# The tail of a decode kernel: down weights in longer runs, and the last 64 rows spread over other transfer engines

## The chip, the cores and the metric

One core of one Trainium2 chip runs the kernel. The metric is device time in microseconds (us) of one execution, median of several. Each timed execution also has a span, from the first to the last instruction that the profile records; the time is 1.7 us or more longer than the span.

The time before was 684.42 us (three runs, 684.41 to 684.58).

## The reference, cut to what matters

One decode step, one token, width 640: adaptive layer norm, attention over a cache of 16,384 positions in 32 heads of 128, then a second layer norm and a gated feed-forward part of width 1,728.

```python
g = silu(h @ w_gate)          # (640) @ (640, 1728)
u = h @ w_up
x = x + gb * ((g * u) @ w_down)   # (1728) @ (1728, 640)
```

The caches are 2 x 32 x 16,384 x 128 bf16, 268 MB of the 290 MB that the kernel reads. Everything else is small, but the feed-forward weights come last, and the output can't be stored until the last row of `w_down` is in and multiplied.

## The kernel before

1,728 = 13 x 128 + 64. The product with `w_down` takes 13 blocks of 128 rows and a rest of 64. Row blocks are loaded in pairs: partition p gets two neighbouring rows of 640 bf16, one run of 2,560 bytes. The columns of gate and up must then be taken in the same order, every second one, so that block j of `gu` meets block j of `w_down`.

```python
NPR = FJ // 2                                    # FJ = 13, FR = 64
wd_cut = [(0, 3), (3, 5), None, (5, NPR), NPR]   # blocks 0-5, 6-9, rest, 10-11, 12
for n, c in enumerate(wd_cut):
    if c is None:
        dst, src = wdr_v[0:FR], B_wd[128 * FJ:F, :]          # 64 rows on partitions 0 to 63
    elif c == NPR:
        dst, src = wd_v[:, 2 * NPR, :], B_wd[256 * NPR:128 * FJ, :]
    else:
        dst = wd_v[:, 2 * c[0]:2 * c[1], :].rearrange("p (q i) n -> p q (i n)", i=2)
        src = B_wd[256 * c[0]:256 * c[1], :].rearrange("(q p i) n -> p q (i n)", p=128, i=2)
    d_wd.append(plan.dma(...))                   # all on the sync queue, after w_gate and w_up
# ... cut: attention output, layer norm, h2 ...
def f_gu(e, wv, ps_t):                           # gate (wv = w_gate), then up (wv = w_up)
    for j in range(FCH):
        for k in range(KC):                      # KC = 5
            if j < 2 * NPR:
                w = wv[:, k, 256 * (j // 2):256 * (j // 2 + 1)].rearrange("p (m i) -> p i m", i=2)[:, j % 2, :]
            else:
                w = wv[:, k, 128 * j:min(F, 128 * (j + 1))]
            r = e.matmul(ps_t[...], lhsT=w, rhs=h2_col[:, k:k + 1], ...)
# ... cut: silu, gu = silu(gate) * up ...
for n, c in enumerate(wd_cut):                   # one PE group for each load, in this order
    o_dn = op(PE, ..., lambda e: f_down(e, js, ...), deps=[o_gum, d_wd[n], o_zf, o_dn])
```

Of the kernel before, what the change touches and what calls it, by code (L numbers as in the profile page):

```python
# [36 lines left out]
class _Plan:  # L37
# [21 lines left out]
    def op(self, eng, pos, fn, deps=(), name=""):  # L59
        o = _Op(eng, pos, fn, list(deps), name, len(self.ops))  # L60
        self.ops.append(o)
        return o
# [89 lines left out]
def build(nc, A_x, A_k, A_v, A_wq, A_wo, B_wg, B_wu, B_wd, c_in, w_mod, out):  # L152
    H, S, Dh = A_k.shape[1], A_k.shape[2], A_k.shape[3]
    D = A_x.shape[2]
    F = B_wg.shape[1]
    KC = D // 128
    TT = S // 128
    FJ = F // 128
    FR = F - 128 * FJ
# [5 lines left out]
    NI = H // 2  # L165
# [14 lines left out]
    with es:  # L180
        block = es.enter_context(nc.Block())
        plan = _Plan(nc, es)
# [17 lines left out]
        wd_v = flat1[:, 2 * KC * F:2 * KC * F + FJ * D].rearrange("p (j n) -> p j n", j=FJ)  # L200
        wdr_v = flat1[:, 2 * KC * F + FJ * D:2 * KC * F + FCH * D]
# [88 lines left out]
        def f_cols(e, v):  # L290
            r = None
            row = cx_row[:, v, :].rearrange("o (m j) -> o j m", j=KC)
            for k in range(KC):
# [6 lines left out]
                  deps=[o_xcol], name="x_f32")  # L300
# [31 lines left out]
        def layernorm_ops(pos, src_f32, src_dep, c0, tag, xc_t):  # L332
# [22 lines left out]
            deps=[o_xc, o_rstd, o_onep], name="t1")  # L355
# [43 lines left out]
        o_fold = [[] for _ in range(NI)]  # L399
# [17 lines left out]
        for i in range(NI):  # L417
# [11 lines left out]
            if 2 * i % G == 0:  # L429
                d_wo[g] = plan.dma(qpos["wo", g], woring[:],  # L430
                                   A_wo[g * G * 128:(g + 1) * G * 128, :].rearrange("(g p) n -> p g n" if lastg else "(p g) n -> p g n", g=G), "wo",
                                   deps=[o_wo[G * g - 1]] if g >= 1 else [], name="dma_wo%d" % g)
            r0 = base - 12.0 if i > 0 else 2.5
            def f_qbc(e, s2=s2, heads=heads):
# [9 lines left out]
                deps=[o_qbcmm[i], o_mult[i - 2] if i >= 2 else None], name="qbc%d" % i)  # L444

            qb = qbc_sb[:, s2].unsqueeze(1).broadcast_to([128, TC, 128])
            for c in range(NC):
# [3 lines left out]
                               deps=[d_k[i], o_qbc[i], o_gm[i - 1] if i >= 1 else None], name="mult%d_%d" % (i, c))  # L451
# [3 lines left out]
                def f_fold(e, sh=sh, ks=ks):  # L455
# [9 lines left out]
                    deps=[o_fold[i][c], o_exp[i - 1] if i >= 1 else None], name="red%d_%d" % (i, c)))  # L465
# [9 lines left out]
            for b in range(2):  # L475
# [3 lines left out]
                    deps=[o_nb[i], o_zrs, o_pvlast[i - NP] if i >= NP else o_zp] + o_red[i], name="exp%d_%d" % (i, b))  # L479
            if last:  # L480
# [9 lines left out]
                               name="dma_v%d_%d" % (i, n)) for n, (a, b) in enumerate(vcut if last else [(0, TP)])]  # L490

            def f_pv(e, j0, j1, i=i, s2=s2, sp=sp, jl=(NG * 3 // 4 if last else NG)):
                r = None
                for j in range(j0, j1):
# [7 lines left out]
                       deps=[o_exp[i], d_v[i][0], o_acc[i - 2] if i >= 2 else (o_xf, o_modc)[i], o_cc], name="pva%d" % i)  # L502
# [3 lines left out]
                          deps=[o_pvb, o_diag[i - 1] if i >= 1 else None], name="acc%d" % i)  # L506

            if not last:

                def f_orow(e, s2=s2, hc=hc):  # L510
# [12 lines left out]
                    deps=[o_rl[i], o_tr[i - 2] if i >= 2 else None], name="O_row%d" % i)  # L523
# [15 lines left out]
                if lastg or heads[1] % G == G - 1:  # L539
                    oc = hc if lastg else slice(heads[1] + 1 - G, heads[1] + 1)  # L540
                    o_on[i] = op(ACT, vbase + 1.2, lambda e, oc=oc: e.activation(out=On[:, oc], in_=OT_ps[:, oc], func=ACTF.Copy),  # L541
                                 deps=[o_tr[i]], name="on%d" % i)
# [34 lines left out]
        QE = float(len(order)) + 1.0  # L577
# [1 line left out]
        d_wu = plan.dma(QE + 0.01, wu_v, B_wu.rearrange("(p k) n -> p k n", k=KC), "wu", deps=[o_fold[NI - 1][-1]], name="dma_wu")  # L579


        NPR = FJ // 2
        wd_cut = [(0, 3), (3, 5), None, (5, NPR), NPR]
        d_wd = []
        for n, c in enumerate(wd_cut):
            if c is None:
                dst, src = wdr_v[0:FR], B_wd[128 * FJ:F, :]
            elif c == NPR:
                dst, src = wd_v[:, 2 * NPR, :], B_wd[256 * NPR:128 * FJ, :]
            else:  # L590
                dst = wd_v[:, 2 * c[0]:2 * c[1], :].rearrange("p (q i) n -> p q (i n)", i=2)
                src = B_wd[256 * c[0]:256 * c[1], :].rearrange("(q p i) n -> p q (i n)", p=128, i=2)
            d_wd.append(plan.dma(QE + 0.02 + 0.01 * n, dst, src, ("wd", n), deps=[o_fold[NI - 1][-1]], name="dma_wd%d" % n))

        o_abf = op(ACT, TE, lambda e: e.activation(out=attn_bf[:], in_=attn_ps[:, 0:KC], func=ACTF.Copy), deps=[o_wo[H - 1]], name="attn_bf")  # L595
# [1 line left out]
                  deps=[o_abf, o_modc], name="ga_attn")  # L597
        o_x1 = op(DVE, TE + 0.2, lambda e: e.scalar_tensor_tensor(
            out=x1[:], in0=tt2[:], scalar=1.0, in1=x_f32[:], op0=ALU.mult, op1=ALU.add, accum_out=st[:, 8:9]),
            deps=[o_ga, o_xf], name="x1")  # L600
# [3 lines left out]
            deps=[o_xc1, o_rstd1, o_onep_b, o_h], name="t2")  # L604
        o_h2 = op(DVE, TE + 1.1, lambda e: e.tensor_tensor(out=h2_col[:], in0=tt1[:], in1=mod_col[:, 3 * KC:4 * KC], op=ALU.add),
                  deps=[o_t2], name="h2_col")
# [4 lines left out]
        def f_gu(e, wv, ps_t):  # L611
            r = None
            for j in range(FCH):
                for k in range(KC):
                    if j < 2 * NPR:
                        w = wv[:, k, 256 * (j // 2):256 * (j // 2 + 1)].rearrange("p (m i) -> p i m", i=2)[:, j % 2, :]
                    else:
                        w = wv[:, k, 128 * j:min(F, 128 * (j + 1))]
                    r = e.matmul(ps_t[0:(128 if j < FJ else FR), j:j + 1], lhsT=w, rhs=h2_col[:, k:k + 1],
                                 start=(k == 0), stop=(k == KC - 1))  # L620
            return r
        o_g = op(PE, TE + 1.2, lambda e: f_gu(e, wg_v, g_ps), deps=[o_h2, d_wg, o_zg], name="gate")
        o_u = op(PE, TE + 1.25, lambda e: f_gu(e, wu_v, u_ps), deps=[o_h2, d_wu, o_zu], name="up")
        o_eg = op(ACT, TE + 1.3, lambda e: e.activation(out=eg[:], in_=g_ps[:, 0:FCH], func=ACTF.Exp, scale=-1.0), deps=[o_g], name="eg")
        o_dg = op(DVE, TE + 1.4, lambda e: e.tensor_scalar_add(out=dg[:], in0=eg[:], scalar1=1.0), deps=[o_eg], name="dg")
# [20 lines left out]
        def f_down(e, js, first, fin):  # L646
            r = None
            for j in js:
                kw = 128 if j < FJ else FR
                wv = wd_v[:, j, :] if j < FJ else wdr_v[0:FR, :]  # L650
                for g in range(4):
                    r = e.matmul(f_ps[32 * g:32 * g + 1, 0:RW], lhsT=gu_col[0:kw, j:j + 1], rhs=wv[:, RW * g:RW * (g + 1)],  # L652
                                 start=(first and j == js[0]), stop=(fin and j == js[-1]), skip_group_check=True)
            return r
        o_dn = None
        for n, c in enumerate(wd_cut):
            js = [FJ] if c is None else ([2 * NPR] if c == NPR else list(range(2 * c[0], 2 * c[1])))
            o_dn = op(PE, TE + 1.8 + 0.01 * n, lambda e, n=n, js=js: f_down(e, js, n == 0, n == len(wd_cut) - 1),
                      deps=[o_gum, d_wd[n], o_zf, o_dn], name="down%d" % n)
        o_t3 = op(DVE, TE + 1.9, lambda e: e.tensor_tensor(out=t3_row[:], in0=f_ps[:, 0:RW], in1=gb_row[:], op=ALU.mult),  # L660
                  deps=[o_dn, o_gbr], name="gb_ffn")
# [8 lines left out]
def bass_adaLN_cond__gqa_block_cached__swiglu_ffn__decode_kernel(  # L670
    nc: bass.Bass,
    A_x: bass.AP,
    A_k_cache: bass.AP,
    A_v_cache: bass.AP,
    A_wq: bass.AP,
    A_wo: bass.AP,
    B_x: bass.AP,
    B_w_gate: bass.AP,
    B_w_up: bass.AP,
    B_w_down: bass.AP,  # L680
    c: bass.AP,
    w_mod: bass.AP,
    out: bass.AP,
):
    build(nc, A_x, A_k_cache, A_v_cache, A_wq, A_wo, B_w_gate, B_w_up, B_w_down, c, w_mod, out)
# [28 lines left out]
```

## Time and profile before

| what | before |
|---|---|
| time, median | 684.42 us |
| span of the profiled execution | 682.7 us |
| moved by the transfer engines | 290.81 MB, 426 GB/s |
| last w_up landing | 672.42 us |
| last w_down landing | 679.04 us |
| output store issued | 680.66 us |

Names in the lines below: PE is TensorE, the matrix engine, PEld its weight loads, DVE is VectorE, SPq the queue of SyncE that issues the loads; `kring` and `vbuf` are buffers that loads fill.

Two lines of the page of the kernel before: the busy share of the 16 transfer engines in 40 slices (9 is 90% or more), and the count of transfer packets by size.

```profile
DMA  9999999999999999999999999999999999999996
...
DMA packets 8082, 290.81 MB, mean 426 GB/s; under 512 B 826, under 2 KB 1532, under 8 KB 3196
```

The kernel is bound by its transfers up to the last slice. A change to the `w_down` loads can only gain in the last 14 us: their first packet starts at 668.46 us. The chain of waits that ended last, in the kernel before (start us, length us, what):

```profile
648.71 28.91 DMA kring<-in_B_w_down_dram
677.62 0.04 issue
677.67 0.73 PE psb L652 x15
678.40 0.14 issue
678.53 0.33 PE psb L652 x3
678.86 0.14 issue
679.00 0.47 PE psb L652 x8
679.46 0.14 issue
679.60 0.33 PE psb L652 x4
```

The chain waits for a `w_down` load that lands at 677.62, then runs four PE groups. The PE instructions of the tail in time order (start, length, line, operation, output and inputs, count, and in brackets the idle time before and what ended it); L619 is up, L652 the product with `w_down`:

```profile
672.47 2.25 PE L619 MATMUL psb<-h_col,kring 128*128 128x1 bf16 x70 [1.87 <-DMA kring<-in_B_w_up_dram]
675.99 0.97 PE L652 MATMUL psb<-kring,gu_col 128*1 128x160 bf16 x24 [1.27 <-DMA kring<-in_B_w_down_dram]
677.67 0.70 PE L652 MATMUL psb<-kring,gu_col 128*1 128x160 bf16 x16 [0.70 <-DMA kring<-in_B_w_down_dram]
678.53 0.30 PE L652 MATMUL psb<-kring,gu_col 64*1 64x160 bf16 x4 [0.16 <-PE psb L652]
679.00 0.43 PE L652 MATMUL psb<-kring,gu_col 128*1 128x160 bf16 x8 [0.16 <-PE psb L652]
679.60 0.30 PE L652 MATMUL psb<-kring,gu_col 128*1 128x160 bf16 x4 [0.17 <-PE psb L652]
```

The first two groups of `w_down` wait for transfers, the last three follow each other with gaps of 0.14 us. The trace also records when each of the 16 engines finished its share of each load. These are the last three of the sixteen (not a view of the page, but the landing records of the trace), and the instruction fetch in the same stretch with the first packets that follow it on its engine:

```
kernel before, landings in us, the three latest engines of 16
w_up               672.29  672.41  672.42
w_down blocks 0-5  674.82  674.83  675.86
blocks 6-9         676.55  676.64  677.62
rest of 64 rows    676.95  677.04  677.83
blocks 10-11       677.60  677.61  678.63
block 12           678.00  678.02  679.04

instruction fetch, 16,384 bytes   672.837 to 673.939
2,560-byte packet                 673.925 to 674.206
2,560-byte packet                 674.192 to 674.472
```

One engine is level with the others when up lands, and 1.03 us behind when the first `w_down` load lands. I call it the straggler. An instruction fetch took 1.10 us of one engine in this stretch, and the first two packets after it take 281 ns each in place of about 104. The trace does not number the engines; that the straggler is the engine of the fetch is tested below (more_130).

Last, three groups of PE matmuls of the kernel before, with one output column each (L555 has two), that differ in the step between the weight columns (busy us, then mean ns of one): L312 has a step of 5 elements, L619 of 2, L555 of 1.

```profile
L312 PE MATMUL psb<-silu_c,vbuf 128*128 128x1 bf16 x150 | 6.2, 178 | 7.1 <-DMA vbuf<-in_w_mod_dram 7.1
...
L619 PE MATMUL psb<-h_col,kring 128*128 128x1 bf16 x130 | 3.8, 165 | 3.7 <-DMA kring<-in_B_w_up_dram 1.9 <-DVE h_col L605 1.9
...
L555 PE MATMUL psb<-P_sb,vbuf 128*128 128x2 bf16 x64 | 1.8, 165 | 2.1 <-DMA vbuf<-in_A_v_cache_dram 2.1
```

The mean length includes the pipeline; the spacing of starts is 40 ns for L312 and 27 ns for the other two. L312 runs at the start of the kernel. L567, also with a step of 5, runs at 664.54 us, between L555 and L619, and has 40 ns too, so the place in the program is not what differs.

### The profile page before, as it was taken

How to read it: one execution, taken by the hardware profiler on the slowest of the kernel's cores; microseconds unless marked ns; L12 is line 12 of the kernel's file. 1: busy time of each engine (PE TensorE's matmuls, PEld its weight loads, DVE VectorE, ACT ScalarE, POOL GpSimd, SP SyncE). 2: the span in 40 equal slices, each digit the busy share in tenths (PEclk: the TensorE clock that was granted, in tenths of full speed). 3: DMA queues.
4: the chain of work that ended last, by engine and by line, in shares of the span. 5: the costliest groups of instructions: out<-in, count | busy, mean ns of one | idle time of the engine just before them, and what ended most of it. 6: DMA issues, size and time to landing. Idle time of an engine off the chain costs nothing.

```text
span 682.7 us, 5209 instructions
## 1 busy us (share of the span) xinstructions
PE 313.0 (46%) x2503; PEld 73.6 (11%) x2055; DVE 485.2 (71%) x254; ACT 55.5 (8%) x206; POOL 9.4 (1%) x30
## 2 busy tenths in 40 slices
PE   1504354554428270644527263462716345255744
PEld 1300010110102010010101001020100101001133
DVE  1029797979696894949589593968949495889901
ACT  1100101010100101010100101010010101001020
POOL 1000000000000000000000000000000000000000
PEclk9957676766858685675758557586755767568975
DMA  9999999999999999999999999999999999999996
GB/s 379 443 427 438 405 447 443 438 442 416 438 430 431 434 443 430 430 427 433 443 430 430 431 426 435 430 430 439 430 434 435 430 434 439 431 434 427 408 423 245
DMA packets 8082, 290.81 MB, mean 426 GB/s; under 512 B 826, under 2 KB 1532, under 8 KB 3196
## 3 DMA queue, kind: packets, MB, share of 16 engines
q1 hardware_dynamic: 8056, 290.48, 98.9%
q8 instruction: 18, 0.29, 0.2%
q14 instruction: 4, 0.03, 0.0%
q10 hardware_dynamic: 4, 0.00, 0.0%
HBM read 290.47 MB, written 0.00 MB: 425 GB/s over the span
## 4 chain that ended last, share of the span: by engine, by line
DMA 60%; DVE 27%; PE 8%; issue 2%; ACT 2%; SPq 1%; POOL 0%; DVEq 0%
DMA kring<-in_A_k_cache_dram 38%; DVE kring L450 17%; DMA vbuf<-in_A_v_cache_dram 14%; DVE kring L452 7%; DMA kring<-in_B_w_down_dram 4%; DMA kring<-in_A_v_cache_dram 4%; PE psb L377 3%; PE psb L496 3%; DVE S_sb L463 2%; PE psb L375 1%; ACT P_sb L476 1%; DVE pm L468 1%; PE psb L567 1%; SPq L71 1%; PE psb L652 0%
## 5 line engine op out<-in xcount | busy, mean ns | idle before, releaser
L450 DVE TENSOR_TENSOR kring<-kring,qbc_sb 128x8192 bf16<-128x8192 bf16 x64 | 282.7, 4418 | 105.6 <-DMA kring<-in_A_k_cache_dram 101.4
L377 PE MATMUL psb<-kring,ident 128*128 128x512 bf16 x448 | 162.7, 525 | 0.0
L452 DVE TENSOR_TENSOR kring<-kring 128x4096 bf16<-128x4096 bf16 x64 | 146.7, 2292 | 2.2
L375 PE MATMUL psb<-kring,ident 128*128 128x512 bf16 x64 | 33.0, 516 | 245.1 <-DVE kring L452 245.1
L496 PE MATMUL psb<-vbuf,P_sb 128*32 128x512 bf16 x944 | 75.0, 473 | 48.2 <-DMA vbuf<-in_A_v_cache_dram 48.1
L463 DVE TENSOR_REDUCE S_sb<-psb 128x64 f32<-128x512 f32 x64 | 43.8, 684 | 35.8 <-PE psb L377 35.8
L496 PEld LDWEIGHTS psb<-vbuf,P_sb 128*32 128x32 bf16 x944 | 26.9, 112 | 151.7 <-issue 84.8
L505 ACT ACTIVATE acc_sb<-psb 128x512 f32<-128x512 f32 x16 | 9.6, 597 | 395.2 <-PE psb L496 395.2
L375 PEld LDWEIGHTS psb<-kring,ident 128*128 128x128 bf16 x64 | 6.4, 101 | 316.7 <-DVE kring L452 306.0
L534 PE MATMUL psb<-ident,O_row 2*32 2x1 bf16 x112 | 4.2, 172 | 35.8 <-ACT O_row L521 35.8
L473 ACT ACTIVATE nb<-gm 64x1 f32<-64x1 f32 x32 | 6.4, 201 | 154.7 <-POOL gm L470 154.3
L476 ACT ACTIVATE P_sb<-S_sb,nb 64x256 bf16<-64x256 f32 x32 | 18.5, 578 | 0.8
L513 PE MATMUL psb<-acc_sb,sel 128*2 128x128 f32 x120 | 15.8, 276 | 0.0
L470 POOL PARTITION_ALL_REDUCE gm<-pm x16 | 5.7, 356 | 619.1 <-DVE pm L468 586.9
L468 DVE TENSOR_REDUCE pm<-S_sb 64x1 f32<-64x256 f32 x32 | 13.2, 414 | 0.8
L596 DVE TENSOR_TENSOR tt<-attn_bf,mod_col 128x5 f32<-128x5 bf16 x1 | 0.2, 165 | 14.2 <-ACT attn_bf L595 14.2
L513 PEld LDWEIGHTS psb<-acc_sb,sel 128*2 128x2 f32 x120 | 9.3, 85 | 2.4
L312 PE MATMUL psb<-silu_c,vbuf 128*128 128x1 bf16 x150 | 6.2, 178 | 7.1 <-DMA vbuf<-in_w_mod_dram 7.1
L567 PE MATMUL psb<-On,woring 128*128 128x1 bf16 x160 | 7.8, 179 | 3.0 <-ACT On L541 2.5
L567 PEld LDWEIGHTS psb<-On,woring 128*128 128x128 bf16 x160 | 7.1, 131 | 3.7 <-ACT On L541 3.2
L534 PEld LDWEIGHTS psb<-ident,O_row 2*32 2x32 bf16 x112 | 3.0, 111 | 38.5 <-ACT O_row L521 38.5
L336 DVE TENSOR_SCALAR xc<-x_f,st 128x5 f32<-128x5 f32 x1 | 0.2, 230 | 9.7 <-POOL st L333 9.7
(89 smaller groups left out, 87.7 us busy)
## 6 DMA issues: line engine op xcount, KB each, us to landing
kring<-in_A_wq_dram SPq DMA_DIRECT2D x1, 5120.0 KB, 26.6
woring<-in_A_wo_dram SPq DMA_DIRECT2D x8, 640.0 KB, 23.9
vbuf<-in_w_mod_dram SPq DMA_DIRECT2D x1, 4800.0 KB, 14.5
vbuf<-in_A_v_cache_dram SPq DMA_DIRECT2D x1, 4096.0 KB, 19.8
vbuf<-in_A_v_cache_dram SPq DMA_DIRECT2D x2, 2048.0 KB, 26.4
kring<-in_B_w_gate_dram SPq DMA_DIRECT2D x1, 2160.0 KB, 20.4
kring<-in_B_w_up_dram SPq DMA_DIRECT2D x1, 2160.0 KB, 25.2
kring<-in_B_w_down_dram SPq DMA_DIRECT2D x1, 960.0 KB, 28.2
```

What stands on the lines that cost most here:

```text
L375: return e.matmul(dst, lhsT=ident[:], rhs=rhs, start=True, stop=fin)
L377: return e.add_instruction(mybir.InstMatmult(name=nc.get_next_instruction_name(), engine=mybir.EngineType.PE, start_tensor_calc=False, sto ...
L450: o_mult[i] = op(DVE, base + 7.0 * c, lambda e, ks=ks, qb=qb: e.tensor_tensor(out=ks, in0=ks, in1=qb, op=ALU.mult), deps=[d_k[i], o_qbc[i] ...
L452: o_f1 = op(DVE, base + 7.0 * c + 4.4, lambda e, ks=ks: e.tensor_tensor(out=ks[:, :, 0:64], in0=ks[:, :, 0:64], in1=ks[:, :, 64:128], op=A ...
L463: o_red[i].append(op(DVE, base + 7.0 * c + 11.5 if c < NC - 2 else base + 7.0 * (NC - 1) + 4.5 + 0.1 * c, lambda e, sh=sh, c=c: e.tensor_r ...
L468: o_mx = op(DVE, eb + 0.1 * b, lambda e, i=i, b=b: e.tensor_reduce(out=pm[half[b], b:b + 1], in_=S_sb[half[b]], axis=AX.X, op=ALU.max), de ...
L476: o_exp[i] = op(ACT, eb + 0.6 + 0.1 * b, lambda e, i=i, b=b, sp=sp: e.activation(out=P_sb[half[b], sp, 0:2 * TP].rearrange("p (t b) -> p b ...
L496: r = e.matmul(acc_ps[s2][q4:q4 + 32, :], lhsT=P_sb[:, sp, 8 * j:8 * j + 32], rhs=vt[i][:, 4 * j:4 * j + 4, :].rearrange("p a d -> p (a d) ...
L505: o_acc[i] = op(ACT, pvb + 0.5, lambda e, s2=s2: e.activation(out=acc_sb[:], in_=acc_ps[s2][:], func=ACTF.Copy), deps=[o_pvb, o_diag[i - 1 ...
L513: r = e.matmul(Or_ps[0:2, 256 * s2:256 * s2 + 128], lhsT=sel[:, 2 * a:2 * a + 2], rhs=acc_sb[:, 128 * a:128 * (a + 1)], start=(a == 0), st ...
L534: r = e.matmul(OT_ps[32 * hq:32 * hq + 32, h - hq + j:h - hq + j + 1], lhsT=O_row[:, s2].rearrange("p (m j) -> p j m", j=G)[:, j, :], rhs= ...
L567: r = e.matmul(attn_ps[:, cc:cc + 1], lhsT=wv[:, cc, :], rhs=On[:, c:c + 1], start=(c == 0 and cc == 0), stop=(c == H - 1 and cc == KC - 1 ...
```

## The change

Units of four rows make runs of 5,120 bytes, and gate and up take every fourth column to match. The loads become blocks 0-3, 4-7, rest, 8-11, 12. The rest of 64 rows is loaded as 56 and 8 rows. The Trainium skill ("DMA: Bandwidth & Descriptors", the section on why a DMA increments its semaphore by 16) says that a transfer uses the largest number up to 16 that divides its slowest dimension, on the lowest-numbered engines: 14 and 8 of them. The last two engines then carry none of the rest.

```diff
-        NPR = FJ // 2
-        wd_cut = [(0, 3), (3, 5), None, (5, NPR), NPR]
+        U = 4
+        NU = FJ // U
+        wd_cut = [(0, 1), (1, 2), None, (2, NU), NU]
...
             if c is None:
-                dst, src = wdr_v[0:FR], B_wd[128 * FJ:F, :]
+                plan.dma(..., wdr_v[0:FR - 8], B_wd[128 * FJ:F - 8, :], ("wd", n), ...)
+                dst, src = wdr_v[FR - 8:FR], B_wd[F - 8:F, :]
...
-                dst = wd_v[:, 2 * c[0]:2 * c[1], :].rearrange("p (q i) n -> p q (i n)", i=2)
+                dst = wd_v[:, U * c[0]:U * c[1], :].rearrange("p (q i) n -> p q (i n)", i=U)
...
-                        w = wv[:, k, 256 * (j // 2):256 * (j // 2 + 1)].rearrange("p (m i) -> p i m", i=2)[:, j % 2, :]
+                        w = wv[:, k, 128 * U * (j // U):128 * U * (j // U + 1)].rearrange("p (m i) -> p i m", i=U)[:, j % U, :]
```

More of the change, by code (lines that the diff above doesn't have):

```diff
@@ L579, in build @@
         d_wu = plan.dma(QE + 0.01, wu_v, B_wu.rearrange("(p k) n -> p k n", k=KC), "wu", deps=[o_fold[NI - 1][-1]], name="dma_wu")
-        NPR = FJ // 2
-        wd_cut = [(0, 3), (3, 5), None, (5, NPR), NPR]
+        U = 4
+        NU = FJ // U
+        assert FJ == U * NU + 1 and FR % 8 == 0
+        wd_cut = [(0, 1), (1, 2), None, (2, NU), NU]
         d_wd = []
@@ L586, in build @@
             if c is None:
-                dst, src = wdr_v[0:FR], B_wd[128 * FJ:F, :]
-            elif c == NPR:
-                dst, src = wd_v[:, 2 * NPR, :], B_wd[256 * NPR:128 * FJ, :]
-            else:
-                dst = wd_v[:, 2 * c[0]:2 * c[1], :].rearrange("p (q i) n -> p q (i n)", i=2)
-                src = B_wd[256 * c[0]:256 * c[1], :].rearrange("(q p i) n -> p q (i n)", p=128, i=2)
+                plan.dma(QE + 0.02 + 0.01 * n, wdr_v[0:FR - 8], B_wd[128 * FJ:F - 8, :], ("wd", n), deps=[o_fold[NI - 1][-1]], name="dma_wdr")
+                dst, src = wdr_v[FR - 8:FR], B_wd[F - 8:F, :]
+            elif c == NU:
+                dst, src = wd_v[:, U * NU, :], B_wd[128 * U * NU:128 * FJ, :]
+            else:
+                dst = wd_v[:, U * c[0]:U * c[1], :].rearrange("p (q i) n -> p q (i n)", i=U)
+                src = B_wd[128 * U * c[0]:128 * U * c[1], :].rearrange("(q p i) n -> p q (i n)", p=128, i=U)
             d_wd.append(plan.dma(QE + 0.02 + 0.01 * n, dst, src, ("wd", n), deps=[o_fold[NI - 1][-1]], name="dma_wd%d" % n))
@@ L614, in f_gu @@
                 for k in range(KC):
-                    if j < 2 * NPR:
-                        w = wv[:, k, 256 * (j // 2):256 * (j // 2 + 1)].rearrange("p (m i) -> p i m", i=2)[:, j % 2, :]
+                    if j < U * NU:
+                        w = wv[:, k, 128 * U * (j // U):128 * U * (j // U + 1)].rearrange("p (m i) -> p i m", i=U)[:, j % U, :]
                     else:
@@ L656, in build @@
         for n, c in enumerate(wd_cut):
-            js = [FJ] if c is None else ([2 * NPR] if c == NPR else list(range(2 * c[0], 2 * c[1])))
+            js = [FJ] if c is None else ([U * NU] if c == NU else list(range(U * c[0], U * c[1])))
             o_dn = op(PE, TE + 1.8 + 0.01 * n, lambda e, n=n, js=js: f_down(e, js, n == 0, n == len(wd_cut) - 1),
```

## The prediction

> **What bounds the kernel now.** The transfers. The page's slices show the 16 transfer engines 90% busy or more in 39 of 40 slices, and 426 GB/s over the span. The change touches only the last 12 us, so only the tail counts. There the chain of waits reads: w_down transfer, landing at 677.62 us, then four short PE groups to 679.93, two VectorE steps, the output store.
>
> The per-engine landing records say more. The up weights land at 672.42 on the last engine and at 672.41 on the next. The first w_down load then lands at 675.86 on the last engine but at 674.83 on the next: one engine is 1.03 us behind and stays so (last load 679.04 against 678.02). An instruction fetch of 16,384 bytes took 1.10 us of one engine from 672.84, which is that lag. The matmuls of w_down wait for this straggler.
>
> **What the change removes, adds, moves.**
> - Bytes: none. Runs of 2,560 bytes become half as many of 5,120. In the trace packets of 2,560 follow each other every 99 ns, those of 5,120 (w_o) every 197.5 ns. So 24 of these in place of 48 save under 0.05 us per engine: nothing.
> - The 64 remaining rows: now 4 packets of 1,280 bytes on each engine, 52 ns each. The Trainium skill ("DMA: Bandwidth & Descriptors", why a DMA increments its semaphore by 16) says that a transfer uses the largest count up to 16 that divides its outer size, and the lowest-numbered engines. So 56 rows go to engines 0-13, four each, 8 rows to engines 0-7, one each, and the last two get none. They save 4 x 52 = 0.21 us; engines 0-7 pay 0.06. I can't read engine numbers in the trace; I guess, at 65%, that the straggler is one of the last two.
> - The boundary of the loads moves: 4, 4, rest, 4, 1 chunks in place of 6, 4, rest, 2, 1. The straggler's landings should become about 675.06, 676.64, rest, 678.22, 678.64.
> - Gate and up weights are read by PE with a step of 4 elements in place of 2. The trace has steps 1 and 2 at 27 ns a matmul and step 5 (L312, L567) at 40 ns. The skill's "SBUF - State Buffer" (DMA port swizzle section) says that two hits in a 16-byte line give full bandwidth: 8 bytes a step is just that. I expect 27 ns. At 40 it would be 70 x 13 = 0.9 us for each matrix; gate hides under the wait for up (1.9 us idle), up does not fully.
>
> **What lies on the critical path.** PE after a landing: 16 matmuls take 0.70 us, 4 take 0.33, gaps 0.14. After: down1 676.69 to 677.39, rest to 677.8, down3 678.27 to 678.97, down4 679.1 to 679.45, against 679.93 now. That is 0.48 us earlier; if the straggler isn't spared, 0.2. Expected gain 0.4 us of 684.4: under 0.1%.
>
> **Prediction: 684.05 us**, 683.6 to 684.6 for 8 in 10. Faster by over 2%: 0.5%; within 2%: 99%; slower: 0.5%.
>
> **What would show it.** Packets of 2,560 bytes gone from the trace, those of 5,120 up by 384, spaced about 197 ns. Last w_down landing about 0.4 us earlier (678.6 in the clock of before). Gate and up still about 27 ns a matmul. The last PE group waits for PE, not for a transfer. Nothing before 646 us changed.
>
> **What would make it wrong.** The instruction fetch falls on another engine or at another moment (up to 1 us either way). The straggler is among engines 0-7, which now carry more. A step of 4 costs as much as 5. The loads of w_down, one more than before, make the sync queue stall. The stream before drifts by some tenths of a us.

## The result, and the profile after

The changed kernel took 684.19 us (median of four, 684.12 to 684.28), the kernel before 684.50 beside it (four, 684.41 to 684.85). The ratio is 0.9995 with a 95% interval of 0.9977 to 1.0012: the same at 2%. (A ratio is the mean time of one kernel's fast runs over that of the other's of the same rounds, so it is not quite the ratio of the medians.) The gain of 0.31 us lies inside that interval; it needs repetition, which follows.

Packets of the changed kernel: 378 fewer than before. 768 packets of 2,560 bytes became 384 of 5,120, and the second load of the rest added 6 semaphore packets.

```profile
DMA packets 7704, 290.81 MB, mean 426 GB/s; under 512 B 832, under 2 KB 1538, under 8 KB 2818
```

The chain that ended last, in the changed kernel. The load waited for is now the one that lands at 678.55, and only two PE groups follow it:

```profile
650.53 28.02 DMA kring<-in_B_w_down_dram
678.55 0.04 issue
678.59 0.73 PE psb L655 x16
679.32 0.14 issue
679.46 0.33 PE psb L655 x4
```

Its PE instructions of the tail. Up takes 2.59 us in place of 2.25, the first `w_down` group waits for `gu` in place of a transfer, the other two groups of 16 wait for transfers, and the groups of 4 (the rest, block 12) start 0.16 us after the group before them:

```profile
672.67 2.59 PE L622 MATMUL psb<-h_col,kring 128*128 128x1 bf16 x70 [1.47 <-DMA kring<-in_B_w_up_dram]
675.59 0.70 PE L655 MATMUL psb<-kring,gu_col 128*1 128x160 bf16 x16 [0.33 <-DVE gu_col L631]
676.82 0.70 PE L655 MATMUL psb<-kring,gu_col 128*1 128x160 bf16 x16 [0.53 <-DMA kring<-in_B_w_down_dram]
677.68 0.30 PE L655 MATMUL psb<-kring,gu_col 64*1 64x160 bf16 x4 [0.16 <-PE psb L655]
678.59 0.70 PE L655 MATMUL psb<-kring,gu_col 128*1 128x160 bf16 x16 [0.61 <-DMA kring<-in_B_w_down_dram]
679.46 0.30 PE L655 MATMUL psb<-kring,gu_col 128*1 128x160 bf16 x4 [0.16 <-PE psb L655]
```

```
changed kernel, landings in us, the three latest engines of 16
w_up               672.28  672.47  672.62
w_down blocks 0-3  674.05  674.19  675.19
blocks 4-7         675.59  675.78  676.77
rest of 64 rows    676.01  676.15  676.98
blocks 8-11        677.36  677.54  678.55
block 12           677.77  677.94  678.95

instruction fetch, 16,384 bytes   672.805 to 673.887
5,120-byte packet                 673.873 to 674.421
```

The straggler is still there. The last landing is at 678.95, only 0.09 us before that of the kernel before (679.04); but up landed 0.20 us later in this trace (672.62 against 672.42), so from the last landing of up it is 6.33 us in place of 6.62. Last landing to output store is 1.57 us (680.52 - 678.95) against 1.62 before.

The group of gate and up matmuls in the changed kernel, to set beside L619 above:

```profile
L622 PE MATMUL psb<-h_col,kring 128*128 128x1 bf16 x130 | 4.5, 171 | 3.3 <-DVE h_col L608 1.9 <-DMA kring<-in_B_w_up_dram 1.5
```

The spacing of starts is 32 ns, not 27.

### The profile page after: what moved, and what is told of

It reads as the page before. It is cut to its first block, busy times and chain, and to the rows that moved or that the text cites. A ratio compares the mean times of both kernels' runs of the same rounds, so it can differ in the third digit from the quotient of the medians.

```text
span 682.6 us, 5210 instructions
## 1 busy us (share of the span) xinstructions
PE 313.9 (46%) x2503; PEld 75.2 (11%) x2055; DVE 485.3 (71%) x254; ACT 55.5 (8%) x206; POOL 9.5 (1%) x30
## 4 chain that ended last, share of the span: by engine, by line
DMA 56%; DVE 31%; PE 7%; issue 3%; ACT 2%; SPq 1%; POOL 0%; DVEq 0%
DMA kring<-in_A_k_cache_dram 38%; DVE kring L450 20%; DMA vbuf<-in_A_v_cache_dram 14%; DVE kring L452 8%; DMA kring<-in_B_w_down_dram 4%; PE psb L377 3%; PE psb L496 2%; DVE S_sb L463 2%; SPq L71 1%; PE psb L375 1%; DVE pm L468 1%; ACT P_sb L476 1%; PE psb L567 1%; POOL gm L470 0%; ACT qbc_sb L442 0%
## 5 line engine op out<-in xcount | busy, mean ns | idle before, releaser
L377 PE MATMUL psb<-kring,ident 128*128 128x512 bf16 x448 | 158.9, 515 | 0.0
L375 PE MATMUL psb<-kring,ident 128*128 128x512 bf16 x64 | 32.4, 507 | 244.8 <-DVE kring L452 244.6
L496 PE MATMUL psb<-vbuf,P_sb 128*32 128x512 bf16 x944 | 78.6, 492 | 47.1 <-DMA vbuf<-in_A_v_cache_dram 47.1
L365 PE MATMUL psb<-kring,h_col 128*1 128x512 bf16 x40 | 4.4, 628 | 5.8 <-DMA kring<-in_A_wq_dram 5.8
```

The costliest lines, as they stand in the source:

```text
L375: return e.matmul(dst, lhsT=ident[:], rhs=rhs, start=True, stop=fin)
L377: return e.add_instruction(mybir.InstMatmult(name=nc.get_next_instruction_name(), engine=mybir.EngineType.PE, start_tensor_calc=False, sto ...
L496: r = e.matmul(acc_ps[s2][q4:q4 + 32, :], lhsT=P_sb[:, sp, 8 * j:8 * j + 32], rhs=vt[i][:, 4 * j:4 * j + 4, :].rearrange("p a d -> p (a d) ...
```

## The experiments

Twelve runs were made, in two further sessions on two chips; two of them repeat the changed kernel and one the kernel before. Kernels of one session share their runs of the kernel before; the second and third groups below are one session. Three quantities are used:

- **time**, and **span**. In 9 and 10 runs of the kernel before, the time exceeded the span by 1.68 to 3.6 us; in 15 runs of the changed kernel by 1.68 to 1.85. So the mean span is the steadier measure of the work. Spans are recorded to 0.1 us, and five runs of one kernel scatter by 0.1 to 0.8.
- **transfer wait**: the mean over all 16 engines of (last w_down landing of the engines) minus the mean of (w_up landing). Being a mean, it does not depend on which engine the instruction fetch hit, as long as one falls into the stretch.
- **PE tail**: from the last landing on any engine to the issue of the output store.

| kernel | run, bytes | rest | time, median | span, mean | transfer wait | PE tail |
|---|---|---|---|---|---|---|
| before (first trace) | 2,560 | 64 | 684.50 | | 5.735 | 1.62 |
| after (first trace) | 5,120 | 56 + 8 | 684.19 | 682.50 | 5.461 | 1.57 |
| *session 2:* before | | | 685.17 (9) | 683.18 | | |
| before_again (1 run) | 2,560 | 64 | 685.48 | 683.5 | 5.754 | 1.61 |
| after_again | 5,120 | 56 + 8 | 684.60 (5) | 682.96 | 5.466 | 1.57 |
| units_only | 5,120 | 64 | 684.88 (5) | 683.08 | 5.560 | 1.57 |
| split_only | 2,560 | 56 + 8 | 684.96 (5) | 683.18 | 5.604 | 1.61 |
| *session 3:* before | | | 684.87 (10) | 683.03 | | |
| after_third | 5,120 | 56 + 8 | 684.65 (6) | 682.90 | 5.482 | 1.57 |
| runs_1280 | 1,280 | 56 + 8 | 684.88 (5) | 683.18 | 5.998 | 1.57 |
| step_one (wrong result) | 5,120 | 56 + 8 | 684.32 (5) | 682.66 | 5.467 | 1.57 |
| more_130 | 5,120 | 56 + 8 | 684.59 (5) | 682.84 | (fetch moved) | 1.79 |
| more_260 | 5,120 | 56 + 8 | 685.17 (5) | 682.88 | 5.507 | 1.76 |
| rest_on_8 | 5,120 | 8 x 8 | 684.69 (4) | 682.90 | 5.837 | 1.57 |
| fine_tail | 5,120 and 2,560 | 56 + 8 | 684.71 (5) | 682.86 | 5.539 | 1.32 |
| rest_on_8_fine_tail | 5,120 and 2,560 | 8 x 8 | 684.87 (5) | 682.70 | 5.874 | 1.39 |

Transfer wait and PE tail come from one profiled execution each. The first three changed-kernel traces, from different sessions, give 5.461, 5.466 and 5.482, so differences of 0.05 us can be read in that column. In the time column they can't.

### Session 2: is the gain real, and which half carries it?

My theory was that the straggler is among engines that carry four packets of the rest in both kernels, so that the split does nothing; the rival, that the split carries all.

**before_again**: no edit. 

> The kernel before once more, for a second trace. In its first trace all engines ran slow for about 0.18 us near 676.3 us (29 packets, 1.5 us over their usual length in sum). Theory A (a chance event, or the two traces' noise): the slow patch is gone or elsewhere, and w_down's last landing on the straggler comes about 6.45 us after the last landing of up, in place of 6.62. Theory B (the shorter runs cause it): the patch is there again. In both the straggler is there, 1.0 us behind the next engine, after an instruction fetch near 672.8.

In the first trace of the kernel before, 29 packets near 676.3 us ran slow, 1.5 us over their usual length in sum. In the second trace there were 8 slow packets there (0.2 us), but 55 near 673.5 (1.6 us). The slow patch moved and did not go away: neither expectation was met as written. (units_only and split_only, below, show what it goes with.) The last landing came 7.09 us after that of up, not 6.45. The transfer wait, the mean of all engines, was the same within 0.02 us (5.754 against 5.735). The straggler was 1.61 us behind, in place of 1.02.

**after_again**: no edit. 

> The changed kernel once more, timed five times beside the others of this job. If the gain of 0.31 us (684.19 against 684.50) is real it is again 0.2 to 0.4 us; if it is noise between runs it lies between -0.1 and 0.15.

684.60 against 685.17: 0.57 us by time, 0.22 us by mean span. The gain came again, though the 95% interval of the ratio (0.9976 to 1.0001) just includes no gain, and its larger part here lies outside the span. More on that under more_260.

**units_only**: the rest back to one load.

```diff
-                plan.dma(..., wdr_v[0:FR - 8], B_wd[128 * FJ:F - 8, :], ...)
-                dst, src = wdr_v[FR - 8:FR], B_wd[F - 8:F, :]
+                dst, src = wdr_v[0:FR], B_wd[128 * FJ:F, :]
```

> Units of four rows and matching columns, the rest of 64 rows left as one load over 16 engines. My theory (the straggler is among engines 8 to 13, which carry four rest packets in both kernels, so the split does nothing): same time as the changed kernel within 0.1 us. Rival (the split carries the gain): the time is that of the kernel before, 0.3 us slower than the changed kernel.

**split_only**: the kernel before with this edit the other way round.

```diff
-                dst, src = wdr_v[0:FR], B_wd[128 * FJ:F, :]
+                plan.dma(..., wdr_v[0:FR - 8], B_wd[128 * FJ:F - 8, :], ...)
+                dst, src = wdr_v[FR - 8:FR], B_wd[F - 8:F, :]
```

> The kernel before with only the rest of 64 rows split into 56 and 8. My theory: no faster than the kernel before (0 to 0.1 us). Rival: 0.2 to 0.3 us faster, as the changed kernel.

By time, units_only was 684.88 and split_only 684.96, both between the two kernels. Neither theory held in full. By mean span they were 683.08 and 683.18, the two kernels 682.96 and 683.18, with runs of one kernel that scatter by 0.1 to 0.5 us, so neither time nor span tells the halves apart. The transfer wait, read from one trace each, does, and so do the packets' own durations after 660 us:

```
mean ns of one packet     2,560 bytes            5,120 bytes
rest in one load of 64    108.3 and 108.4        205.1
rest as 56 + 8            105.6                  201.0, 201.2, 201.5
```

Both halves act on the transfer wait. Longer runs (with the new boundaries of the loads, which came along; runs_1280 below changes the run length alone) shorten it from 5.745 to 5.560 (0.185 us) with the rest in one load, and from 5.604 to 5.470 with the rest split. That fits the packets: successive packets of one engine start about 3 ns before the previous one ends, so 48 x 105.4 = 5.06 us become 24 x 202.1 = 4.85. The split shortens it by 0.09 (5.560 to 5.470) or 0.14 (5.745 to 5.604). This is not because an engine has fewer packets, since the mean over the engines counts the same 64. The row packets that run at the same time become quicker: 48 x 2.75 ns = 0.13 us, and 24 x 3.9 ns = 0.09 us.

Why do the row packets suffer from the rest? The Trainium skill ("SBUF - State Buffer", the section on the DMA port swizzle) says that partitions 0 to 63 reach only 8 of 16 ports, and the rest lies on partitions 0 to 63. With 16 engines writing there, two of them would share a port and each would meet an engine that is still writing rows. With the split, two engines are out of it. The trace agrees in time. In units_only the early engines start on the rest at 671.8 to 672.2 and the late ones at 674.8 to 675.5 us, and just then and after it row packets are slow: 27 take over 210 ns from 672 to 673 and 25 from 675 to 676 (0.75 and 1.09 us over 198 ns in sum). In the three traces of the changed kernel they are 3 to 10 and 4 to 12 (0.10 to 0.29 and 0.16 to 0.34 us). With runs of 2,560 it is the same: packets over 112 ns from 672.8 to 673.8 and from 675.8 to 676.8 are 32 and 25 in the first trace of the kernel before, 73 and 3 in the second, but 7 and 1 in split_only. So the slow patch of before_again goes with the rest in one load and not with the run length. Why it does so is not shown: the ports remain an explanation, since no run put the rest on other partitions.

The straggler's number can be narrowed from the changed kernel's landings. It has only one landing of the rest, 0.21 us after its second load (676.98 after 676.77), which is 4 x 52 ns. By the rule of the skill, engines 0 to 7 would show two, and 14 and 15 none. So it is one of engines 8 to 13, which carry four packets before and after.

### Session 3: run length, weight step, fetches

**runs_1280**: one row for each partition and run.

```diff
-        U = 4
-        NU = FJ // U
-        wd_cut = [(0, 1), (1, 2), None, (2, NU), NU]
+        U = 1
+        NU = FJ - 1
+        wd_cut = [(0, 4), (4, 8), None, (8, NU), NU]
```

> The changed kernel with runs of 1,280 bytes (one row a partition, gate and up columns contiguous), same boundaries of the loads. From the spacings in the traces (52 ns a packet of 1,280, 197.5 a packet of 5,120) the twelve row blocks take 96 x 52 = 4.99 us on each engine in place of 24 x 197.5 = 4.74: the last w_down landing comes 0.25 us later after that of up, and the time is 0.2 to 0.3 us over the changed kernel. Rival (the run length does not matter at this size, the gain is only in the boundaries of the loads and in chance): within 0.1 us.

0.23 us slower than the changed kernel by time, 0.28 by span, as expected; the ranges of the times overlap (684.56 to 685.31 and 684.43 to 684.85). The transfer wait grew by twice that, 5.998 against 5.482, in a profiled execution that was the slowest of the five (span 683.6). Short runs cost more than their shortest spacing tells: packets of 1,280 bytes averaged 58.3 ns in this tail against 55 undisturbed.

**step_one**: columns of gate and up contiguous (relative error 1.3). Its output is wrong, which doesn't matter for the time.

```diff
-                        w = wv[:, k, 128 * U * (j // U):128 * U * (j // U + 1)].rearrange("p (m i) -> p i m", i=U)[:, j % U, :]
+                        w = wv[:, k, 128 * j:128 * (j + 1)]
```

> The changed kernel with gate and up columns read contiguously: the result is wrong on purpose (the columns no longer match the rows of w_down). Matmuls of gate and up go back from 32 to 27 ns, so gu is ready 0.35 us earlier. My theory: the matmuls of the second w_down load wait for the straggling engine anyway, so the time stays within 0.1 us. Rival (the step of 4 gives back part of the gain): 0.3 us faster.

Gate and up return to 27 ns a matmul. The group in step_one:

```profile
L622 PE MATMUL psb<-h_col,kring 128*128 128x1 bf16 x130 | 3.8, 165 | 3.7 <-DVE h_col L608 1.9 <-DMA kring<-in_B_w_up_dram 1.8
```

The tail in step_one: up is done 0.34 us sooner, and the second group of `w_down` then waits 0.77 us for the transfer, where it waited 0.53 in the changed kernel.

```profile
672.76 2.25 PE L622 MATMUL psb<-h_col,kring 128*128 128x1 bf16 x70 [1.83 <-DMA kring<-in_B_w_up_dram]
675.73 0.70 PE L655 MATMUL psb<-kring,gu_col 128*1 128x160 bf16 x16 [0.72 <-DMA kring<-in_B_w_down_dram]
677.21 0.70 PE L655 MATMUL psb<-kring,gu_col 128*1 128x160 bf16 x16 [0.77 <-DMA kring<-in_B_w_down_dram]
```

So in this trace the quicker matmuls only lengthen a wait. The five times say something else: 684.32 against 684.65, spans 682.66 against 682.90, about what the rival expected. The profiled execution was the slowest of the five (span 683.0, the other four 682.5 to 682.7), so its trace need not stand for them. Whether the step of four costs time stays open: 0.2 to 0.3 us by the times, nothing by the one trace, and no cause seen.

**more_130** and **more_260**: matmuls repeated in the idle start, with their results unchanged, to move the places at which PE's instructions are fetched. The number in the name counts PE instructions, a weight load and a matmul each.

```diff
+        o_ccol = op(PE, 0.15, lambda e: [f_cols(e, 0) for _ in range(13)][-1], deps=[d_c, o_ones, o_ccol], name="more_cols")
```

(26 in place of 13 for more_260; each call of `f_cols` makes five matmuls.)

> The changed kernel with 65 more matmuls (130 PE instructions with their weight loads) in the idle start, results unchanged, so that PE's stream reaches the points at which 16,384 bytes (256 instructions of 64) are fetched 130 instructions sooner: the fetch near 672.8 us should move to about 669, in gate, and the one at 679 or 680 to about 675. Theory (a fetch costs its transfer engine 1.1 us and slow packets after it, some 1.4 in all): the straggler of the first w_down load is gone or is one engine of the up load, and an engine falls back after 675. Time within 1 us either way. Rival (the fetch is not the cause): the same straggler in the first w_down load, same time.

> The same with 130 more matmuls (260 instructions), so the fetches stay at their places in the tail but there is one more early. If successive fetches go to successive transfer engines, the fetch near 672.8 hits another engine than before: by the landings 4 of 16 engines are 2.5 us ahead and can take 1.4 us for nothing, and then the last landing comes 1.0 to 1.5 us sooner; if it hits one of the later ones, nothing changes. If a fetch's engine depends on its place and not its number: same straggler, same time within 0.1 us.

The fetches belong to PE: the kernel has 18 of 16,384 bytes for 2,503 + 2,055 = 4,558 matmuls and weight loads, 64.7 bytes each. With 260 more there were 19.

```
landings in us, the three latest engines; fetches in us
changed kernel (third)  up 672.21 672.37 672.50   first w_down load 673.78 674.07 675.51   fetches 666.66, 672.90, 679.39
more_130                up 672.38 672.39 674.04   first w_down load 673.94 673.97 675.61   fetches 670.76, 676.88
more_260                up 672.27 672.48 673.73   first w_down load 674.11 675.30 675.37   fetches 666.56, 673.12, 684.60
```

With 130 instructions more the fetch came at 670.76, and its engine fell back 1.65 us already in the load of up. The straggler of the changed kernel, in the first `w_down` load, is thus the engine that the fetch hit: when the fetch moved, the lag moved with it. The fetches came later than expected (670.76 and 676.88, not 669 and 675), and the second one left no second straggler: the last engine but one had its last landing at 677.69, as in the changed kernel (677.84). The time did not change (684.59 against 684.65). Up's matmuls now start at 674.09, and PE works off all the groups of `w_down` without a wait:

```profile
674.09 2.58 PE L623 MATMUL psb<-h_col,kring 128*128 128x1 bf16 x70 [3.02 <-DMA kring<-in_B_w_up_dram]
677.00 0.70 PE L656 MATMUL psb<-kring,gu_col 128*1 128x160 bf16 x16 [0.34 <-DVE gu_col L632]
677.87 0.70 PE L656 MATMUL psb<-kring,gu_col 128*1 128x160 bf16 x16 [0.17 <-PE psb L656]
678.74 0.30 PE L656 MATMUL psb<-kring,gu_col 64*1 64x160 bf16 x4 [0.17 <-PE psb L656]
679.20 0.70 PE L656 MATMUL psb<-kring,gu_col 128*1 128x160 bf16 x16 [0.17 <-PE psb L656]
680.07 0.30 PE L656 MATMUL psb<-kring,gu_col 128*1 128x160 bf16 x4 [0.16 <-PE psb L656]
```

In more_260 the two fetches of the tail fell at their old places, but the earlier one hit one of the late engines: the gate weights landed at 668.71 on the last engine, 1.37 us after the next one. In the third trace of the changed kernel the two are at 667.23 and 667.07. Two engines were behind at the end. So in this one trace the engine went with the number of the fetch and not with its place in the program. The hoped-for hit on an engine that is ahead did not come.

more_260 shows a second thing. Its time rose by 0.5 us while its span did not (682.88 against 682.90). In its trace the last fetch is at 684.60, after the span's end. Of the other thirteen traces, all but two have their last fetch at 680.5 or before, and their time exceeds the span by 1.68 to 1.84. In rest_on_8_fine_tail it came at 684.48, and in before_again none is recorded after 673.11 where the others have one near 680; their time exceeds the span by 2.42 and 1.98, and more_260's by 2.27. The kernel before shows such an excess (2.0 us and more) in 7 of its 19 runs of sessions 2 and 3, the changed kernel in none of its 15 runs of all sessions. So a part of its gain by time seems to be that a fetch no longer falls into the end of the program. That the late fetch is what lengthens the time is inferred from these coincidences; no run forced it.

### The rest on eight engines, and a finer tail

**after_third**: no edit, the control. 

> The changed kernel once more, as a control beside the three that follow: 0.2 to 0.4 us under the kernel before. In its traces the straggler shows one landing for the rest of 64 rows, 0.21 us after its second w_down load, so it is one of engines 8 to 13.

684.65 against 684.87: 0.22 us, 0.13 by span.

**rest_on_8**: eight loads of 8 rows.

```diff
-                plan.dma(..., wdr_v[0:FR - 8], B_wd[128 * FJ:F - 8, :], ...)
+                for m in range(FR // 8 - 1):
+                    plan.dma(..., wdr_v[8 * m:8 * m + 8], B_wd[128 * FJ + 8 * m:128 * FJ + 8 * m + 8, :], ...)
```

> The changed kernel with all 64 remaining rows in eight loads of 8 rows, so on engines 0 to 7 alone (8 packets of 1,280 each in place of 5). My theory (the straggler is one of engines 8 to 13 and carries 4 of these packets now): the straggler saves 4 x 52 = 0.21 us, engines 0 to 7 get 0.21 more but have 1.0 us to spare; last w_down landing and time 0.2 us earlier. Rival (the straggler is among engines 0 to 7, or chance outweighs it): no gain, or 0.2 us later.

The straggler did save its 0.21 us: from its second load to its last landing it took 1.97 us (677.41 to 679.38), against 2.18 in after_third (677.08 to 679.26). That fits engines 8 to 13. But the last landing was no earlier. The row packets slowed down, from 201.5 to 219.0 ns in the mean, and the transfer wait rose from 5.482 to 5.837. Up too landed later, at 673.06. Eight rows at a time lie on eight neighbouring partitions, two ports by the skill's table, so this is the direction the port explanation asks for. Time 684.69, against 684.65: no gain.

**fine_tail**: the third unit in two halves, the rest's matmuls joined to the first half's.

```diff
-        wd_cut = [(0, 1), (1, 2), None, (2, NU), NU]
+        wd_cut = [(0, 1), (1, 2), None, "h0", "h1", NU]     # h0: blocks 8, 9; h1: blocks 10, 11
...
+            elif c in ("h0", "h1"):
+                dst = wd_v[:, j0 + i0:j0 + i0 + 2, :]        # j0 = 8, i0 = 0 or 2
+                src = B_wd[128 * j0:128 * U * NU, :].rearrange("(p i) n -> p i n", i=U)[:, i0:i0 + 2, :]
```

> The changed kernel with the third unit of four rows loaded as two halves (runs of 2,560) and the rest's matmuls joined to the first half's. Theory (after the last landing PE still works off the 16 matmuls of a load that landed 0.4 us before): the wait from last landing to the output store falls from 1.57 to about 1.35 us, time 0.2 us under the changed kernel. Rival (the last landing alone counts): same time.

The PE tail fell to 1.32 us, as expected. The end of fine_tail:

```profile
678.47 0.66 PE L660 MATMUL psb<-kring,gu_col 64*1 64x160 bf16 x12 [0.30 <-DMA kring<-in_B_w_down_dram]
679.30 0.44 PE L660 MATMUL psb<-kring,gu_col 128*1 128x160 bf16 x8 [0.17 <-DMA kring<-in_B_w_down_dram]
679.90 0.30 PE L660 MATMUL psb<-kring,gu_col 128*1 128x160 bf16 x4 [0.16 <-PE psb L660]
```

But the span fell by 0.04 us only, and the time rose by 0.06. The transfer wait was 0.06 longer, and in the profiled execution the straggler was 1.65 us behind in place of 1.42. The PE tail's gain is shown. What gave it back is only partly seen: of 0.25 us, 0.06 went to a longer transfer wait, about what the runs of 2,560 in the third unit should cost by the packet means above (16 x 102.7 ns in place of 8 x 198.5). The straggler's lag, which varies from 1.0 to 1.7 us between traces, may cover the rest; that stays open.

**rest_on_8_fine_tail**: both edits. 

> Both: 0.4 us under the changed kernel, 0.7 us under the kernel before, if the two terms add. If chance in the stream before (some tenths of a us) is larger than both, it can't be told from the two alone.

The shortest mean span of the session with a right result (682.70, 0.20 us under the changed kernel, where 0.4 was expected), but the time was 684.87, because it exceeded the span by 1.79 to 2.67 us. No version with a right result beats the changed kernel by time, beyond the 0.06 us of more_130.

## Why the prediction was right or wrong

684.05 us was predicted, with 683.6 to 684.6; 684.19 came out. The gain predicted was 0.37 us from the median (the text rounds it to 0.4). Measured were 0.31, 0.57 and 0.22 us in three sessions. That 684.19 came within 0.14 us of the forecast is in part luck. By mean span the gain was 0.22 and 0.13 us (sessions 2 and 3), which is nearer to the 0.2 that the prediction gave for a straggler that isn't spared, and it was not spared; the remainder of the gain by time lies outside the span, where the prediction had no term. The steps were right in part.

1. **"What bounds the kernel now: the transfers", with one straggler after a fetch: right.** more_130 moved the fetch and the straggler moved with it. The term was under-sized: the fetch costs its engine not only 1.10 us. The first packets after it take 548 ns in place of 198, or 2 x 281 in place of 2 x 104, another 0.35. Some 1.4 us in sum is near the lags of 1.0 to 1.7 us; that of the first trace, 1.03, would fit an engine that had been about 0.4 us ahead, which is not shown.
2. **"So 24 of these in place of 48 save under 0.05 us per engine: nothing": wrong in size.** It saved 0.13 to 0.19 us of transfer wait (units_only, split_only, and the changed kernel). I had taken the spacing of undisturbed packets, 99 and 197.5 ns. In this tail packets of 2,560 bytes last 108.3 ns in the mean and those of 5,120 205.1 or 201, each some 3 ns more than its spacing.
3. **"I guess, at 65%, that the straggler is one of the last two": wrong.** It is one of engines 8 to 13 and carried four packets of the rest before and after. The 0.21 us never came from there. Yet the split was worth 0.09 to 0.14 us of transfer wait, by a route that the prediction did not name: row packets run quicker while fewer engines write the rest. Alone it did not shorten the mean span of the kernel before (683.18 and 683.18).
4. **The landings "about 675.06, 676.64, rest, 678.22, 678.64": right but for the guess.** Measured 675.19, 676.77, 676.98, 678.55, 678.95. The first two are 0.13 late, the last two 0.3, which is the rest's 0.21 us more. So the check that it named, a last landing at about 678.6, 0.4 us earlier, failed: it came 0.09 us earlier.
5. **"I expect 27 ns" for a step of four elements: wrong, 32 ns.** Up took 2.59 us in place of 2.25. The prediction's rule, two hits in a line give full bandwidth, is the skill's. By the trace `gu` is ready at 675.53, well before the second load at 676.77, so the cost is hidden there. By the five times of step_one it may not always be.
6. **The order of the end: mostly right.** "The last PE group waits for PE, not for a transfer": yes, the group of block 12 (down4) starts 0.14 us after that of blocks 8-11 (down3). The PE tail is shorter by about 0.045 us (1.61 to 1.57) in every trace with the load boundaries of the changed kernel and the straggler at its place, units_only and runs_1280 included, but not in split_only. Last landing to the last matmul's end was 0.84 us, where 0.81 had been reckoned.
7. **The sync queue does not stall: right.** It issued the last `w_down` load by 651.36, before by 660.94. Neither matters, since the first landing is at 670 or later.

So the sum came out near although terms were wrong in both directions: 0.21 us of the straggler that weren't there, against run length and split that were worth more than nothing and a part outside the span. What was in nobody's account is the time outside the span, in which the kernel before lost up to 1.9 us in some runs.

## What to carry to other kernels

When all engines finish a queue of equal loads, look at the landing of each engine and not at the load's. One engine held up for some 1.4 us by an instruction fetch set the end here, and packets saved on the other fifteen buy nothing directly. Cost small packets by their mean in the crowded stretch, not by their best spacing. And for gains under a thousandth compare spans and landing means beside the time: here the scatter of the time outside the span was larger than the whole effect.

## What the Trainium skill lacked or had wrong

- **"SBUF - State Buffer", the DMA port swizzle section (the note on 16-byte lines).** It says that two hits in a line give full bandwidth and counts a stride of up to 8 bf16 elements as free. As weights of a matmul with one output column, columns with a step of 4 bf16 elements (8 bytes, two hits) took 32 ns a matmul, against 27 ns at steps 1 and 2 and 40 ns at step 5; step_one, which changes this alone, brought the 27 ns back. The free range ended between 2 and 4.
- **"DMA: Bandwidth & Descriptors", queues and rings.** It names row 14 as the one for refills. Here the large instruction fetches (16,384 bytes, one for some 250 PE instructions) ran on queue 8 by the trace's numbering, and only those of 8,192 bytes on queue 14. No page says what a fetch costs the other transfers: in these traces its packet lasts 0.88 to 1.31 us on one of the 16 engines, and the next packets in the tail were 0.35 us slow in sum.
- **"DMA: Bandwidth & Descriptors", specifications (at least 512 bytes for line rate).** Far above 512 bytes the run length still counted in this tail: the same blocks took 6.00 us in runs of 1,280, 5.60 in runs of 2,560 and 5.47 in runs of 5,120 (all with the rest split, other loads included).
- **The same page, how the engine count is chosen.** The counts of 14 and 8 agree with the trace (two immediate marks, 22 with data). It gives no figure for what a 64-partition load on all 16 engines costs the loads beside it: packets of 2,560 bytes averaged 108.4 ns beside it and 105.6 beside 56 + 8 rows.
- **No page has it:** the time of an execution can exceed the span of its instructions by 1.7 to 3.6 us, and in the traces at hand the larger values went with a last instruction fetch after the span's end (684.5 us) or not recorded at all.
